# Attention, routed experts and an MLP in one kernel: expert 0's place cut from 160 to 128 rows, and the order of the loads behind it

## The chip, the cores and the metric

One core of a Trainium2 chip runs the whole program. The metric is device time in microseconds of one execution, the median of three runs; the profile is one further execution of the same program, with times in microseconds from the start of its span.

## What is computed

Three stages follow each other. Causal attention with a decay runs over 2 batches of 8 heads, 576 positions and 64 columns. A gate then sends each of the 1152 tokens to one of 8 experts, an MLP of 512 to 1024 to 512 with a relu, and an expert keeps its first 288 tokens. A last MLP of 512 to 2048 to 512 runs over all tokens.

```python
scores = np.where(causal, -1000000000.0, scores + decay)
attn = np.exp(scores - max); attn = attn / (sum + 1e-09)
x = attn @ v                                    # 1152 tokens of 512
expert_idx = np.argmax(x @ w_gate, axis=1)      # 8 experts, capacity 288
h = np.maximum(np.einsum('ecd,edf->ecf', disp, w1), 0.0)
y = np.einsum('ecf,efd->ecd', h, w2)            # out[i] = gate_w[i] * y
h = x @ w_in                                    # then the last MLP
g = np.where(h >= 1, h, np.where(h <= -1, 0.0, (h + 1) ** 2 / 4))
out = g @ w_out
```

With the inputs that the reference draws the gate gives the eight experts 89, 168, 151, 69, 104, 79, 131 and 361 tokens; expert 0 has 89.

## The kernel before

**Attention** (lines 411 to 938) is a loop over steps t, each of which works on several heads at once; a string of operations (ORDER) fixes the order on every engine. In step t the score columns of head t + 1 are made (cols_part, lines 534 to 552: two matmuls, an exp on ACT, and on POOL the mask of the diagonal block, line 551), and head t is multiplied with v (av_part, line 588), which reads the masked blocks of the step before. The helper at line 525 sends a row of corrections through a small DMA, which the matmul at line 547 reads one step later.

**The token buffer.** disp lies in DRAM and holds CAPS rows per expert. It is filled with zeros first: in step t the pieces 2t - 2 and 2t - 1 of 128 rows are written from an SBUF tile (lines 887 to 889), as many pieces as E * CAPS / 128. CAPS comes from the table of places (lines 69 to 75), where RW is the largest number of tokens that can be left over at one place. Then the tokens are scattered into it with indirect DMAs of POOL (scatter, line 729): five for batch 0 in steps 11 to 15, five for batch 1 after the attention.

**The places.** PLACES lists, in the order in which the experts are worked, the rank by size and the rows of a place. Place 0 is always expert 0, whose tokens don't go through disp: perm (line 721; 80 PE matmuls in the trace, two for each f32 product) picks them with one-hot matrices of C0 columns, C0 being the rows of place 0, and lines 935 and 937 copy the result from PSUM into XT. The tokens of the others are read back from disp by x_load (four DMAs, line 407) and turned around by x_trans (DVE, lines 1026 and 1030; for places over 160 rows, "split" ones, ACT makes a rounded copy at line 1031 and DVE or POOL the rest at line 1032).

**The experts** (expert, lines 1139 to 1178). A place goes through eight quarters of weights of 512 KB each. In the four quarters of w1, eight blocks of PSUM columns are made, and ACT writes each through a relu into hf (line 1100), so that one of four PSUM banks is free again. The four quarters of w2 go in eight half products (PARTS); the third of these is the first to read the blocks 4 to 7 of hf. In places of up to 160 rows the matmul at line 1045 reads the weights as they were loaded, in f32; the trace shows 64 matmuls for w1 and 64 for w2 in such a place. x_trans of the next place stands between the blocks of w1 if that place is split (after blocks 1, 3, 5 and 7), else between the half products of w2.

**The loads.** All weights go through the queue of SP, in the order of a list (loads, line 176), each as soon as one of 13 buffers is free: eight RAW and, after the attention, five ST. Eight quarters of place 0 are loaded into RAW during the attention. The list also holds the weights of the last MLP, "m" loads of 512 KB; the first of them stands behind the seventh quarter of place 1, and its conversion, three DVE steps at lines 962, 965 and 968, is tied by m_step to blocks 0, 2 and 4 of place 1. SP works strictly in order, and x_load waits in it until the scatter has landed.

```python
        pump()                                   # line 1093
                if i == 0:                       # lines 1153 to 1156, in expert(e)
                    x_fetch(1)
                if r == 3:
                    x_fetch(e + 2)
```

Of the kernel before, what the change touches and what calls it, by code (L numbers as in the profile page):

```python
# [10 lines left out]
F32 = mybir.dt.float32  # L11
# [4 lines left out]
ACTF = mybir.ActivationFunctionType  # L16
# [8 lines left out]
def most_over(places, n):  # L25
    best = 0
    for m in range(1 << len(places)):
        over = [p for p in range(len(places)) if m >> p & 1]
        need = sum(places[p][1] + 1 for p in over if p == 0)
        for r in range(len(places) - 1):  # L30
            need += max([places[p][1] + 1 for p in over if p and places[p][0] >= r], default=0)
        if need <= n:
            best = max(best, len(over))
    return best
# [3 lines left out]
def attention_moe_mlp_kernel(  # L38
# [14 lines left out]
    nc = tc.nc  # L53
# [6 lines left out]
    KD = DM // 128  # L60
# [3 lines left out]
    KF = 8  # L64
# [1 line left out]
    NG = 3  # L66
    GW = N // NG
    GT = GW // 128
    PLACES = ((7, 160), (6, 128), (0, 288), (5, 128), (1, 224), (4, 128), (2, 192), (3, 160))
    CP = [c for _, c in PLACES]  # L70
    C0, CMAX = CP[0], max(CP)
    PS = [sum(CP[:p]) for p in range(E + 1)]
    LEFT = [min(cap, N // (r + 1) if p else N) - c for p, (r, c) in enumerate(PLACES)]
    RW = max(LEFT) // 32 * 32
    CAPS = max([c + RW for c, o in zip(CP, LEFT) if o > 0] + CP)
    NK = most_over(PLACES, N)
    XW = max([min(N, PS[p]) + CP[p] for p in range(E)] + [N + RW])
    THREE = 256
    SPLIT = [c > 160 for _, c in PLACES]
    NHL = 5  # L80
# [19 lines left out]
    xt_p = ctx.enter_context(tc.tile_pool(name="xtp", bufs=1))  # L100
# [32 lines left out]
    def build_tables(pos_c):  # L133
# [4 lines left out]
        for e in range(E):  # L138
            nc.gpsimd.memset(place_c[:, e], float(PLACES[e][0]))
            nc.gpsimd.memset(cap_c[:, e:e + 1], float(CP[e]))  # L140
# [10 lines left out]
    def quarter_src(i):  # L151
        p, r = divmod(i, 8)
        w = (w1, w2)[r // 4]
        if p == 0:
            return w1[E, r] if r < 4 else w2[0, r - 4]
        return w[bass.ds(at_place(p), 1), r % 4].rearrange("e p f -> (e p) f")
# [3 lines left out]
    def at_place(p):  # L160
        if p not in places:
            places[p] = nc.sync.value_load(ord_i[0:1, p:p + 1], min_val=0, max_val=E - 1)
        return places[p]
# [18 lines left out]
    def pump(n=99):  # L182
        while n and free and loads:
            _, kind, i = loads.popleft()
            t = raws[kind, i] = free.popleft()
            if kind == "w":
                src = quarter_src(i)
            elif kind == "m":
                t, src = t.bitcast(U32), (w_in, w_out)[i % 2][i // 2].bitcast(U32)
            else:  # L190
                src = more_src(i)
            nc.sync.dma_start(out=t, in_=src)
            n -= 1
# [204 lines left out]
        nc.vector.tensor_tensor(out=order_sb, in0=ps[:, NT:], in1=ge[:, 0, 0:NT], op=ALU.add)  # L398

    xrs, xts, x_next = {}, {}, []  # L400
    XT = xt_p.tile([128, KD, C0], F32, tag="xt", name="XT")

    def x_load(e, src):
        n = src.shape[0] // 32
        xrs[e] = x_next[e % 2 if e < E else 1]
        for j in range(DM // 128):
            nc.sync.dma_start(out=xrs[e][32 * j:32 * j + 32, 0:n],
                          in_=src[:, 128 * j:128 * j + 128].rearrange("(t p) d -> p t d", p=32))


    with ExitStack() as actx:
# [179 lines left out]
        def norm_scale(h):  # L591
            o = AV[h % 2][:, :, (h % 2) * (NV - VC):(h % 2) * (NV - VC) + VC]
            r = sm_p.tile([128, IB], F32, tag="r", name="r")
            nc.vector.tensor_scalar(out=r, in0=o[:, :, D + E], scalar1=1e-9, scalar2=None, op0=ALU.add)
            nc.vector.reciprocal(out=r, in_=r)
            return o, r.unsqueeze(2)
# [120 lines left out]
        def perm(b, ibs, ks=range(KD)):  # L717
            for ib in ibs:
                n = min(128, S - ib * 128)
                for k in ks:  # L720
                    nc.tensor.matmul(px[k][:, 0:C0], xss[b][:n, ib, 2 * k:2 * k + 2].rearrange("p h d -> p (h d)"),
                                     sel[b, ib][:n].bitcast(F32), start=((b, ib) == (0, 0)),
                                     stop=((b, ib) == (NB - 1, IB - 1)))

        def scatter(b, ibs):
            si, xs = sis[b], xss[b]
            for ib in ibs:
                n = min(128, S - ib * 128)
                nc.gpsimd.indirect_dma_start(
                    out=disp_v[b * IB + ib], out_offset=bass.IndirectOffsetOnAxis(ap=si[:n, ib:ib + 1], axis=0),  # L730
                    in_=xs[:n, ib].rearrange("p h d -> p (h d)"), in_offset=None,
                    bounds_check=E * CAPS - 1, oob_is_err=False)
# [149 lines left out]
        for t in range(-AHD, NH + 1):  # L882
# [24 lines left out]
            if t == HB + 6:  # L907
                px = [next(s1), next(s1), next(s2), next(s2)]
                s2_free = next(s2)
        o, r = norm_scale(NH - 1)  # L910
# [19 lines left out]
        for k in range(KD):  # L930
            perm(1, range(3, IB), (k,))
        xts[0] = XT
        for k in range(KD):
            if k % 2:
                nc.vector.tensor_copy(out=XT[:, k], in_=px[k][:, 0:C0])
            else:
                nc.scalar.activation(out=XT[:, k], in_=px[k][:, 0:C0], func=ACTF.Copy)
        scatter(1, range(IB))
        bases_gen = compact_bases()

# [34 lines left out]
    def m_step(h):  # L975
        while m_at and m_at[0] <= h:
            m_at.pop(0)
            next(conv)
# [32 lines left out]
    with ExitStack() as mctx:  # L1011
        mp = mctx.enter_context(tc.tile_pool(name="moe", bufs=1))
        x_next.extend(mp.tile([128, max(CP[2 - i::2] + [RW]) // 32, 128], F32, name=f"xn_r{i}")
                      for i in range(2))
        xn = mp.tile([128, KD, 2, CMAX], F32R, name="xn")
        hf = mp.tile([128, KF, C0], F32, name="hf")
        xT0 = mp.tile([128, CMAX], F32, name="xT0")

        def x_trans(e, k, n, split):
            if k == 0:  # L1020
                xts[e] = xn if split else XT if e < E else (
                    x_next[0].rearrange("p t d -> p (t d)")[:, 0:KD * n].rearrange("p (k n) -> p k n", n=n))
# [67 lines left out]
        def more_src(i):  # L1090
            return (w1, w2)[i % 8 // 4][bass.ds(more_e[i // 8], 1), i % 4].rearrange("e p f -> (e p) f")

        pump()
        hx = mp.tile([128, KF, 2, CMAX], F32R, name="hx")
        tp = mctx.enter_context(tc.tile_pool(name="sum", bufs=2))
        invert = invert_slots(px[3][:, 32:32 + 2 * (N // 128)], tp)
# [37 lines left out]
        def x_fetch(e):  # L1134
            if e < E:
                x_load(e, disp.rearrange("(e c) d -> e c d", c=CAPS)[bass.ds(at_place(e), 1), 0:CP[e]]
                       .rearrange("e c d -> (e c) d"))

        def expert(e):
            x, n, split = xts.pop(e), CP[e], SPLIT[e]  # L1140
            for r in range(4):
                i = e * 8 + r
                for fi in range(2):
                    fc = r * 2 + fi
                    ps = bank(ph_ring, n, split)
                    for k in range(KD):
                        c = slice(k * 256 + fi * 128, k * 256 + fi * 128 + 128)
                        product(ps, (hls if split else raws)["w", i], c, operand(x, k, n, split), k == 0, k == KD - 1)
                    hidden(ps, fc, n, split, 2 * i + fi)
                    w_step(2 * i + fi)  # L1150
                    if e + 1 < E and SPLIT[e + 1] and 2 * r + fi in XUP:
                        x_trans(e + 1, XUP.index(2 * r + fi), CP[e + 1], True)
                if i == 0:
                    x_fetch(1)
                if r == 3:
                    x_fetch(e + 2)
                extra(i)
                done("w", i)
            yb = {}
            for s, (d, f0, f1) in enumerate(PARTS):  # L1160
                i = e * 8 + 4 + d
                if f0 == 0:
                    yb[d] = bank(py_ring, n, split)
                for fc in range(f0, f1):
                    c = slice(fc * 128, fc * 128 + 128)
                    product(yb[d], (hls if split else raws)["w", i], c, operand(hx if split else hf, fc, n, split), fc == 0, fc == KF - 1)
                if f1 == KF:
                    token(yb[d], d, n, *bases[e])
                z = 2 * e * 8 + 8 + s
                w_step(z)  # L1170
                m_step(z)
                for k in range(KD):
                    if e + 1 < E and not SPLIT[e + 1] and s == XAT[k]:
                        x_trans(e + 1, k, CP[e + 1], False)
                if s % 2:
                    extra(z // 2)
                if f1 == KF:
                    done("w", i)

        for e in range(E - 2):  # L1180
            expert(e)
        for _ in plan:
# [179 lines left out]
```

## Time and profile before

| | |
|---|---|
| median of three runs | 486.29 us (486.25 to 486.47) |
| the profiled execution | 486.1 us, span 484.4 us, granted clock 0.987 |
| PE busy | 467.2 us, 96% |
| DVE, ACT, POOL busy | 306.0, 257.9, 153.3 us |
| attention with the picking of expert 0's tokens | to 130.4 us |
| place 0, place 1 | 130.4 to 147.9 us, 147.9 to 162.1 us |
| places 2 to 7 | to about 280 us |
| last MLP | to the end |

A busy share says only how full an engine was. What a change of one stage is worth is read from the stage: which engine has no gap in it, and which wait ends last where there is one.

### The profile page before, as it was taken

The page shows a single profiled execution, that of the slowest core. Times are in us where ns is not written, and L with a number is a line of the kernel's source. Part 1 is how long each engine was busy: PE and PEld are TensorE (multiplying, and loading weights), DVE is VectorE, ACT ScalarE, POOL GpSimd, SP SyncE. Part 2 cuts the span into 40 slices and gives each one's busy share as a digit, 9 for nine tenths or more (in the row PEclk, how much of TensorE's full clock was granted, in tenths as well). Part 3 has the DMA queues.
Part 4 walks back from the last instruction along what each step waited for, and adds up shares of the span by engine and source line. Part 5 has one row for each costly group of instructions (what it writes and reads, how often), then busy time and mean ns, then how long its engine had stood idle before and what let it go on. Part 6 is the DMA issues. An engine that isn't in the chain of part 4 may idle for free. (4 is left out here: it accounts for less than half of the span.)

```text
span 484.4 us, 8905 instructions
## 1 busy us (share of the span) xinstructions
PE 467.2 (96%) x3054; PEld 430.3 (89%) x3054; DVE 306.0 (63%) x778; ACT 257.9 (53%) x579; POOL 153.3 (32%) x242
## 2 busy tenths in 40 slices
PE   6799999999999999999998999999999999999995
PEld 2499998999899999999997999999999999999994
DVE  8657768844415666757566268887878554755532
ACT  8867776764224642673561354545455455566650
POOL 7867866763302380292190220000000000400002
PEclk9889999999999999999998999999999999999999
DMA  7558998921569985978970554333300000300001
GB/s 211 164 167 266 321 303 283 292 77 44 170 251 355 369 322 156 354 278 262 300 279 7 207 188 150 118 126 128 127 1 0 1 0 2 130 2 0 1 0 65
DMA packets 38576, 78.46 MB, mean 162 GB/s; under 512 B 14103, under 2 KB 19175, under 8 KB 38524
## 3 DMA queue, kind: packets, MB, share of 16 engines
q1 hardware_dynamic: 37020, 73.19, 45.7%
q0 software_dynamic: 1456, 4.57, 2.4%
q8 instruction: 26, 0.43, 0.4%
q14 instruction: 26, 0.21, 0.1%
q10 hardware_dynamic: 48, 0.06, 0.0%
HBM read 67.36 MB, written 10.49 MB: 161 GB/s over the span
## 5 line engine op out<-in xcount | busy, mean ns | idle before, releaser
L1000 PE MATMUL PB<-x2h,HL 128*128 128x384 f32 x192 | 64.9, 338 | 0.0
L1002 PE MATMUL PB<-x2h,HL 128*128 128x384 f32 x192 | 64.6, 336 | 0.0
L1001 PE MATMUL PB<-x2l,HL 128*128 128x384 f32 x192 | 64.4, 336 | 0.0
L588 PE MATMUL PB<-VT,pt 128*128 128x102 f32 (+2 forms) x480 | 60.5, 262 | 0.0
L588 PEld LDWEIGHTS PB<-VT,pt 128*128 128x128 f32 (+2 forms) x480 | 55.1, 175 | 3.9
L1269 DVE SCALAR_TENSOR_TENSOR PB<-PB,s 128x384 f32<-128x384 f32 x48 | 27.2, 566 | 48.5 <-ACT s L1267 45.9
L1284 PE MATMUL PB<-HL,gh 128*128 128x512 f32 x144 | 56.6, 393 | 0.0
L1283 PE MATMUL PB<-HL,gh 128*128 128x512 f32 x144 | 56.4, 392 | 0.0
L1285 PE MATMUL PB<-HL,gl 128*128 128x512 f32 x144 | 56.0, 389 | 0.0
L1266 ACT ACTIVATE s<-PB 128x384 f32<-128x384 f32 x48 | 23.6, 492 | 56.5 <-PE PB L1002 55.7
L548 ACT ACTIVATE pt<-PB 128x288 f32<-128x288 f32 (+2 forms) x96 | 35.7, 391 | 25.3 <-PE PB L547 22.6
L1290 POOL DMA_INDIRECT out_dram<-ST,order_sb x6 | 6.0, 997 | 133.1 <-DVE ST L1289 131.6
L514 DVE CUSTOM_DVE_ANT_0 dump<-PB,msk 128x128 f32<-128x128 f32 (+1 forms) x64 | 30.9, 490 | 21.7 <-PE PB L508 19.1
L1270 ACT ACTIVATE gh<-PB 128x384 fp32r<-128x384 f32 x48 | 23.6, 492 | 32.8 <-DVE PB L1269 31.7
L1000 PEld LDWEIGHTS PB<-x2h,HL 128*128 128x128 f32 x192 | 36.1, 188 | 1.8
L1001 PEld LDWEIGHTS PB<-x2l,HL 128*128 128x128 f32 x192 | 36.0, 188 | 1.8
L1002 PEld LDWEIGHTS PB<-x2h,HL 128*128 128x128 f32 x192 | 36.0, 188 | 0.0
L508 PE MATMUL PB<-KB,QM 128*128 128x128 f32 (+2 forms) x96 | 31.8, 348 | 3.9 <-DVE KB L796 3.2
L1272 DVE TENSOR_TENSOR gl<-PB,gh 128x384 fp32r<-128x384 f32 x48 | 26.8, 558 | 13.4 <-ACT gh L1270 13.4
L546 PE MATMUL PB<-QA,KA 128*128 128x288 f32 (+2 forms) x96 | 31.1, 327 | 1.4 <-ACT pt L548 1.1
L1285 PEld LDWEIGHTS PB<-HL,gl 128*128 128x128 f32 x144 | 27.0, 188 | 6.0
L997 DVE TENSOR_TENSOR HL<-wc,HL 128x512 fp32r<-128x512 f32 x40 | 27.0, 719 | 7.9 <-ACT HL L996 7.9
(295 smaller groups left out, 1125.3 us busy)
## 6 DMA issues: line engine op xcount, KB each, us to landing
RAW<-in_w_dram SPq DMA_DIRECT2D x40, 512.0 KB
ST<-in_w_dram SPq DMA_DIRECT2D x24, 512.0 KB
qk<-in_qkT_dram SPq DMA_DIRECT2D x15, 576.0 KB
RAW<-in_w_in_dram SPq DMA_DIRECT2D x12, 512.0 KB
disp<-zero SPq DMA_DIRECT2D x22, 256.0 KB
RAW<-in_w_out_dram SPq DMA_DIRECT2D x9, 512.0 KB
ST<-in_w_out_dram SPq DMA_DIRECT2D x7, 512.0 KB
VT<-in_v_dram SPq DMA_DIRECT2D x8, 320.0 KB
```

Of the source, the lines that this page charges most:

```text
L508: nc.tensor.matmul(s[:n, :w - a], QM[h % 2][:, ib * 128:ib * 128 + n], KB[i][:, a:w], start=True, stop=True)
L514: nc.vector.tensor_tensor_reduce(out=dump[:n, :w - a], in0=s[:n, :w - a], in1=msk[:n, m0:m0 + w - a], scale=1.0, scalar=NEG if r < IB else ...
L546: nc.tensor.matmul(s[:n, :z - a], KA[i][:, js], QA[i][:, iss], start=True, stop=False)
L548: nc.scalar.activation(out=pt[:n, POFF[jb] + a:POFF[jb] + z], in_=s[:n, :z - a], func=ACTF.Exp, scale=0.125)
L588: nc.tensor.matmul(o[:n, ib, ws], pt[:m, c0:c0 + n], v[:m, jb].rearrange("p a b -> p (a b)")[:, vs], start=(jb == 0), stop=(jb == ib))
L1000: nc.tensor.matmul(ps, wh, ah, start=first, stop=False)
L1001: nc.tensor.matmul(ps, wh, al, start=False, stop=False)
L1002: nc.tensor.matmul(ps, wl, ah, start=False, stop=last)
L1269: nc.vector.scalar_tensor_tensor(out=ps, in0=ps, scalar=1.0, in1=s, op0=ALU.max, op1=ALU.min)
L1283: nc.tensor.matmul(o, gh[:, c], wh, start=(fc == 0), stop=False)
L1284: nc.tensor.matmul(o, gh[:, c], wl, start=False, stop=False)
L1285: nc.tensor.matmul(o, gl[:, c], wh, start=False, stop=(fc == NF2 - 1))
```

## The change

Place 0 has 128 rows in place of 160. XT and hf keep the size of 160 columns, for place 7. Of the loads that the queue takes when the ST buffers become free, only three are issued first (the quarters 0 to 2 of place 1), then the tokens of place 1, then those of place 2, and only then the other two quarters; the reads of the tokens out of the loop of place 0 are dropped.

```diff
-    PLACES = ((7, 160), (6, 128), (0, 288), (5, 128), (1, 224), (4, 128), (2, 192), (3, 160))
+    PLACES = ((7, 128), (6, 128), (0, 288), (5, 128), (1, 224), (4, 128), (2, 192), (3, 160))
     CP = [c for _, c in PLACES]
-    C0, CMAX = CP[0], max(CP)
+    C0, CMAX, CF = CP[0], max(CP), max(c for c in CP if c <= 160)
...
-    XT = xt_p.tile([128, KD, C0], F32, tag="xt", name="XT")
+    XT = xt_p.tile([128, KD, CF], F32, tag="xt", name="XT")
...
-                nc.vector.tensor_copy(out=XT[:, k], in_=px[k][:, 0:C0])
+                nc.vector.tensor_copy(out=XT[:, k, 0:C0], in_=px[k][:, 0:C0])
             else:
-                nc.scalar.activation(out=XT[:, k], in_=px[k][:, 0:C0], func=ACTF.Copy)
+                nc.scalar.activation(out=XT[:, k, 0:C0], in_=px[k][:, 0:C0], func=ACTF.Copy)
...
-        hf = mp.tile([128, KF, C0], F32, name="hf")
+        hf = mp.tile([128, KF, CF], F32, name="hf")
...
-        pump()
+        pump(3)
...
-                if i == 0:
-                    x_fetch(1)
-                if r == 3:
+                if r == 3 and e:
                     x_fetch(e + 2)
...
+        x_fetch(1)
+        x_fetch(2)
+        pump()
         for e in range(E - 2):
             expert(e)
```

The table also sets RW, and through it CAPS. Before, the largest rest was 128 (the capacity of 288 less 160 at place 0), so RW was 128 and CAPS 224 + 128 = 352, which makes 22 pieces of zeros. Now the largest rest is 288 - 128 = 160, CAPS is 384, and there are 24 pieces. The last two fall in step 12, and the first scatter is in step 11.

SP's queue in steps 11 and 12 of the attention, before (disp is the token buffer, ct the row of corrections; DMASW is a semaphore of a scatter, DMAHW of a DMA of SP):

```order
L889 DMA disp<-zero 128x512 [waits DMAHW5_49]
L525 DMA QB_151<-ct 1x5x128 [waits DMAHW6_49,Activation_49]
L467 DMA VT_160<-in_v_dram 128x10x64 [waits DMAHW7_49,PE_49]
L525 DMA QB_152<-ct 1x5x128 [waits DMAHW0_49,Activation_49]
L162 TENSOR_LOAD ord_i [waits DVE_49]
```

and now:

```order
L889 DMA disp<-zero 128x512 [waits DMAHW5_49]
L525 DMA QB_151<-ct 1x5x128 [waits DMAHW6_49,Activation_49]
L467 DMA VT_160<-in_v_dram 128x10x64 [waits DMAHW7_49,PE_49]
L889 DMA disp<-zero 128x512 [waits DMAHW0_49,DMASW0_49]
L889 DMA disp<-zero 128x512 [waits DMAHW1_49]
L525 DMA QB_152<-ct 1x5x128 [waits DMAHW2_49,Activation_49]
L162 TENSOR_LOAD ord_i [waits DVE_49]
```

Two writes of zeros stand ahead of the row of corrections, and the first waits for a scatter. On POOL the same stretch reads now (before, the second L729 waited for ACT alone):

```order
L496 TENSOR_TENSOR QB_152<-qk,QA_144 64x576 [waits Activation_49,Pool_49]
L551 AFFINE_SELECT pt<-pt 128x128 [waits Activation_49] x4
L551 AFFINE_SELECT pt<-pt 64x64 [waits Activation_49]
L729 DMA disp<-xs,si 3072x512 [waits DMAHW1_49,DMAHW0_49,Activation_49]
L471 COPY VT_160<-vwall 128x10x8
```

The second scatter waits for the two writes of zeros (DMAHW0 and DMAHW1), and behind it in POOL's order stand the copy into VT and the masks of the next head.

SP's queue behind the attention, now (xn_r of 32x4x128 are the tokens of place 1, of 32x9x128 those of place 2; in_w_dram is an expert's weights, in_w_in_dram the first m load):

```order
L192 DMA ST_1752<-in_w_dram 128x1024 [waits DMAHW5_49]
...
L407 DMA xn_r_1781<-disp 32x4x128
...
L407 DMA xn_r_1780<-disp 32x9x128
...
L192 DMA ST_1753<-in_w_dram 128x1024 [waits DMAHW6_49]
L192 DMA ST_1754<-in_w_dram 128x1024 [waits DMAHW7_49]
L192 DMA RAW_100<-in_w_dram 128x1024 [waits DMAHW0_49,PE_49]
L192 DMA RAW_101<-in_w_dram 128x1024 [waits DMAHW1_49,PE_49]
L192 DMA RAW_102<-in_w_in_dram 128x1024 [waits DMAHW2_49,PE_49]
L192 DMA RAW_103<-in_w_dram 128x1024 [waits DMAHW3_49,PE_49]
```

Before, five ST loads stood ahead of the tokens of place 1, then two RAW loads and the m load, and only then the tokens of place 2. So between the tokens of place 1 and the m load there were two loads, and now there are the tokens of place 2 and four loads.

The order of DVE in place 1 is the same in both programs (now):

```order
L1127 TENSOR_TENSOR x2l<-PB_74,x2h 128x128 [waits Activation_49]
L236 TENSOR_TENSOR mm<-at,base_f 128x64
L239 TENSOR_REDUCE bx<-mm 128x8 [waits DVE_49]
L962 TENSOR_SCALAR wc_1763<-RAW_102 128x512 [waits DMASW6_49,DMASW7_49,DMASW5_49,DMAHW2_49,DMASW1_49,DMASW0_49]
L1030 STREAM_TRANSPOSE xT_1784<-xn_r_1780 128x288 [waits DMAHW5_49,DMAHW4_49,DMAHW3_49]
L1032 TENSOR_TENSOR xn<-xT_1784,xn 128x288 [waits Activation_49]
```

The first step on the m load (L962, of RAW_102) stands ahead of the first turning of place 2's tokens (L1030).

## Rows read from the trace of the kernel before

**Rows 1.** The page's line of engines: busy us (share of the span) and instructions.

```profile
PE 467.2 (96%) x3054; PEld 430.3 (89%) x3054; DVE 306.0 (63%) x778; ACT 257.9 (53%) x579; POOL 153.3 (32%) x242
```

**Rows 2.** Waits of PE from 30 us on: us in total, times, longest.

```profile
PE PB L1045 <- PEq L1228: 2.2, 1, 2.2
PE PB L508 <- DVE STAT L514: 0.4, 1, 0.4
```

**Rows 3.** PE's timeline, places 0 and 1: start us, us, engine, line, operation, count.

```profile
130.40 8.96 PE L1045 MATMUL PB<-XT,RAW 128*128 128x160 f32 x64
139.20 8.86 PE L1045 MATMUL PB<-hf,RAW 128*128 128x160 f32 x64
147.89 7.31 PE L1045 MATMUL PB<-XT,ST 128*128 128x128 f32 x64
```

**Rows 4.** Stretches: length; busy (count) of PE, PEld, DVE, ACT, POOL; clock; DMA share; GB/s.

```profile
117.29:120.57 3.28, 3.28 (x26) 3.25 (x25) 2.33 (x14) 1.61 (x7) 0.00 (x0) 1.00 0.00 1
130.40:147.89 17.49, 17.49 (x130) 17.49 (x129) 4.26 (x23) 3.34 (x11) 1.38 (x2) 1.00 0.79 286
147.89:162.10 14.21, 14.21 (x131) 14.21 (x129) 10.82 (x26) 8.00 (x21) 2.79 (x4) 1.00 1.05 368
```

**Rows 5.** POOL's timeline in steps 11 to 13 (in brackets the idle time before).

```profile
100.39 1.17 POOL L729 DMA_INDIRECT disp<-xs,si  x1 [0.29 <-POOL QB L496]
104.50 0.99 POOL L729 DMA_INDIRECT disp<-xs,si  x1 [0.59 <-ACT ct L524]
105.68 0.33 POOL L551 TENSOR_SCALAR_AFFINE_SELECT pt<-pt 128x128 f32<-128x128 f32 x1
```

**Rows 6.** The scatter issued at 104.50 us, by itself.

```profile
DMA to landing us min/median/max: 2.8/2.8/2.8
```

**Rows 7.** A stretch of step 13, columns as in rows 4.

```profile
105.00:106.00 1.00, 1.00 (x10) 0.97 (x8) 0.86 (x3) 0.98 (x3) 1.00 (x3) 1.00 0.06 20
```

**Rows 8.** SP's timeline (x is the number of DMAs in the row).

```profile
93.64 0.92 SPq L889 DMA_DIRECT2D disp<-zero  x2
125.77 2.53 SPq L192 DMA_DIRECT2D ST<-in_w_dram  x5
139.17 1.89 SPq L407 DMA_DIRECT2D xn_r<-disp  x4
143.58 1.87 SPq L407 DMA_DIRECT2D xn_r<-disp  x4
```

**Rows 9.** PE's timeline, step 14: the product with v that follows the first score columns.

```profile
109.36 0.36 PE L588 MATMUL PB<-VT,pt 128*128 128x102 f32 x2
```

**Rows 10.** The last scatter: POOL's timeline, and its landing by itself.

```profile
131.18 0.91 POOL L729 DMA_INDIRECT disp<-xs,si  x1 [0.30 <-issue]
...
DMA to landing us min/median/max: 7.7/7.7/7.7
```

**Rows 11.** Stretches behind the attention, columns as in rows 4.

```profile
131.00:137.00 6.00, 6.00 (x46) 6.00 (x45) 1.10 (x7) 1.52 (x5) 0.91 (x1) 1.00 1.02 406
139.00:140.00 1.00, 1.00 (x9) 1.00 (x8) 0.00 (x0) 0.30 (x1) 0.00 (x0) 1.00 0.00 0
147.00:150.00 3.00, 3.00 (x27) 3.00 (x26) 1.15 (x4) 0.65 (x3) 0.00 (x0) 1.00 1.17 236
```

**Rows 12.** DVE's timeline in place 1.

```profile
149.24 0.43 DVE L962 TENSOR_SCALAR wc<-RAW 128x512 uint32<-128x512 uint32 x1
150.54 0.69 DVE L1030 STREAM_TRANSPOSE xT<-xn_r 128x288 f32<-128x288 f32 x1 [0.88 <-DMA xn_r<-disp]
```

**Rows 13.** ACT's timeline in place 1.

```profile
151.27 0.44 ACT L1031 ACTIVATE xn<-xT 128x288 fp32r<-128x288 f32 x1 [1.06 <-DVE xT L1030]
155.86 0.45 ACT L1100 ACTIVATE hf<-PB 128x128 f32<-128x128 f32 x2 [0.16 <-ACT xn L1031]
```

**Rows 14.** Stretches around PE's one long gap, columns as in rows 4.

```profile
257.46:259.70 2.24, 0.01 (x1) 0.03 (x1) 2.17 (x7) 0.33 (x1) 0.00 (x0) 1.00 0.01 4
260.55:263.96 3.41, 3.41 (x14) 2.83 (x13) 1.23 (x3) 0.47 (x2) 0.00 (x0) 0.50 0.01 2
```

## The prediction, made before the changed kernel was run

> **What bounds the kernel now.** I read the page's line of engines first, to see whether one engine is the bound: PE is busy 467.2 us, 96% of the span [rows 1]. The waits of PE come next, to see what it ever waits for: from 30 us on there is one wait of 2.24 us and one of 0.4 [rows 2]. So a matmul that gets shorter counts in full, unless something that was hidden comes late; a change here is judged by what it makes late. PE's timeline of places 0 and 1 shows streams without a hole, 64 matmuls for each of w1 and w2 [rows 3], at full clock [rows 4]. Then I follow the two queues that the change rearranges: POOL and SP in attention steps 12 and 13 [rows 5, 8], and SP, DVE and ACT behind the attention [rows 8, 12, 13].
>
> The sum is made against the profiled execution, 486.1 us; the median of the runs is 486.29, about 0.2 above it, which is added at the end. A difference under 0.2%, about 1 us, can't be told from none.
>
> **The gain.** Place 0 takes 17.49 us for 128 matmuls of 160 columns, 136.6 ns each, and place 1 takes 14.21 us for 128 of 128 columns, 111.0 ns [rows 4]. The difference, 25.6 ns, times 128 is 3.3 us. In the picking of expert 0's tokens 26 matmuls take 3.28 us [rows 4], 126 ns each; a fifth of that is 25 ns, times 80 is 2.0 us. PE is full in both stretches, so the gain is **-5.3 us** if nothing comes late. The copies into XT shrink with the columns, some hundredths of a microsecond, taken as nothing. Expert 0 has 89 tokens, so its rest stays empty in both programs.
>
> **Cost 1: two more writes of zeros, in the attention.** CAPS grows to 384, and the writes of zeros of step 12 wait for scatter 0, as the order of SP shows. That scatter was issued at 100.39 [rows 5]. How long it takes has no row of its own here; another one took 2.8 us and the last one, beside weight loads, 7.7 [rows 6, 10], so it lands between 103.2 and 108.1. I take 106, the middle, since in its stretch one load and the end of the zeros share the DMA engines. The pair of writes then takes 0.92 us to issue [rows 8], the second about 0.5 behind the first, and lands 2.6 us after its issue at about 109.1; that is a little under the 2.8 us of a transfer of the same 256 KB [rows 6], for hardly anything else moves then, 20 GB/s [rows 7]. The second scatter on POOL waits for both. It can go at about 109.4 and not at 104.50 [rows 5], 4.9 us late, and the copy and the masks stand behind it. The first mask went at 105.68 for 0.33 us; 4.9 later it ends at 110.9. PE wants it for the product with v at 109.36 [rows 9]. So PE stands still for about **+1.7 us** (with the scatter at 103.2: 0, since the mask would end at 108.1; with it at 108.1: 3.8). The row of corrections that stands behind the writes in SP's queue goes out at about 107.1 and not before the first score columns of step 14 need it by much; its lateness lies inside the same 1.7 us. Batch 0's later scatters and the masks behind them are late by the same amount at first, and POOL has idle time in each step to catch up; I cost that at nothing.
>
> **Cost 2: the m load behind the tokens of place 2.** In SP's queue the reads of the tokens wait for the last scatter, issued at 131.18, landed 7.7 us later, at 138.9 [rows 10]; SP went on at 139.17 [rows 8], 0.3 behind. While it waited the queue moved 406 GB/s [rows 11]: five ST loads and the scatters. Now two loads of 512 KB fewer stand there, 1.05 MB / 406 GB/s = 2.6 us, and the picking is some 0.6 us shorter up to that scatter, so it lands at 135.7, counted on the old clock of the attention (bounds: neither helps, 138.3; both and the shorter picking in full, 133.4). The tokens of place 1 are issued from 136.0, for 1.9 us, and those of place 2 start at 138.2 [rows 8]. Their first bytes come 1.4 us after that; this is an estimate from the stretch behind the issue at 139.17, in which nothing has moved yet by 140.00 [rows 11]. Their 590 KB take 2.5 us at the 236 GB/s at which the tokens went before [rows 11]. Five loads follow, the fifth of them the m load, at 524 KB / 406 GB/s = 1.29 us each, 6.5 in all. So the m load lands at 148.6.
>
> This estimate of the link rests on the 406 GB/s of the trace. The Trainium skill, DMA: Bandwidth & Descriptors, Where 436 GB/s comes from, says that a transfer from HBM to SBUF is bound at the HBM side, at some 358 GB/s. By that rule each load would take 1.46 us, the m load would come 0.9 us later, and the sum would be 0.9 us higher; the trace moves 406 here, and the measurement decides.
>
> Before, the m load was there when DVE reached line 962 at 149.24, in place 1's first matmuls, and the first turning of place 2's tokens came at 150.54, held by those tokens [rows 12]. Now the tokens come early and the m load late. Place 1 starts 5.3 us earlier, at 142.6, and its six first blocks of w1, 7.31 us / 8 = 0.89 a block at their rate [rows 3], are done at 147.9. Only four banks exist: the seventh block needs the bank of the third, which ACT empties behind the copy of line 1031 [rows 13], which needs DVE's turning of line 1030, which stands behind line 962. DVE can do line 962 at 148.6, for 0.43 us, and the turning at 149.0. Before, the last block of w1 was emptied 5.8 us after the turning (150.54 to 155.86 + 0.45 [rows 12, 13]); the third of the eight half products reads it. Six half products of 0.89 us are 5.3. So place 1 ends at about 149.0 + 5.8 + 5.3 = 160.1, where it ended at 162.10 [rows 4] and would end at 156.8 with the gain alone. This costs **+3.3 us**, and one for one with the landing of the scatter (bounds +1.0 and +5.9). PE's first gap there is about 2.4 us, from 147.9 to ACT's emptying at some 150.3. If the attention is late by cost 1, the scatter, the m load and place 1 all move by that, and nothing is counted twice. Later weights are asked for in the same order, and place 2 keeps its tokens; I cost the rest at nothing, since PE ran without a wait from place 2 to 257 us before [rows 2].
>
> **The clock.** After PE's one long gap, 2.24 us, the granted clock is 0.50 for 3.41 us, and 14 matmuls run there [rows 14]. At half the full 2.4 GHz the stretch does half its work, so it costs 1.7 us. The 0.4 us gap was not followed by that. The two new gaps, 1.7 and 2.4 us, stand near the one that was; I count one such stretch, **+1.7 us** (bounds 0 and 3.4).
>
> **Sum.** -5.3 + 1.7 + 3.3 + 1.7 = +1.4; 486.1 + 1.4 = 487.5, and 0.2 for the median: **487.7 us**.
>
> **The rivals.**
> - *Both waits, no stretch at half clock*: -5.3 + 1.7 + 3.3 = -0.3, 486.0 us. For it: the gaps may be shorter than estimated, or fall where the chip does not answer. Chance 0.25.
> - *Both gaps are followed by one*: 487.7 + 1.7 = 489.4 us. Chance 0.10.
> - *Faster, since the m load isn't late*: it decides whether the last scatter lands by about 133 instead of 135.7. Its 7.7 us [rows 10] against the 2.8 of one by itself [rows 6] say that the loads in the queue hold it; with two fewer it could gain more than their own time. Then only cost 1 is left and with it perhaps a stretch at half clock: -5.3 + 1.7 = -3.6, 482.7, or 484.4 us. Against it: three loads still stand ahead. Chance 0.15.
> - *Faster, since the zeros don't hold POOL*: if scatter 0 lands at 103.5 or before, the masks are in time. Then -5.3 + 3.3 = -2.0, 484.3 us, or 486.0 with a stretch. Chance 0.13, a third of it with the stretch.
> - *Neither is late*: 486.3 - 5.3 = 481.0 us. Chance 0.07.
> - *The change doesn't do what it says*: expert 0 would overflow its 128 rows and go through the rest's loop; with 89 tokens it can't here. No chance is given to it.
>
> **How the numbers follow.** The forecast has 0.30. Faster by over 1 us: 0.15 + 0.08 + 0.07 = 0.30. The same: 0.25 + 0.05 = 0.30. Slower: 0.30 + 0.10 = 0.40. The forecast's own range, with the landing of the scatter 1 us either way, is 486.7 to 488.7. The range for 8 in 10 leaves out the case in which neither is late and most of that of two stretches: 482.6 to 489.0.
>
> **What would show it.** PE's timeline of place 0 should show 64 matmuls in about 7.3 us; if not, the gain fails. In the waits of POOL the second scatter should stand at about 109 with a wait for the writes of zeros, and PE should wait at line 588 for the masks. In place 1 DVE should wait at line 962 for the m load, PE at line 1045 for ACT's relu, and the windows should show a granted clock of 0.50 behind one of the gaps. The forecast is wrong if place 1's m load is in RAW before its first blocks are done, if POOL's second scatter goes at about 104, or if no stretch at half clock follows.

## The result, and the profile after

The changed kernel takes **489.30 us** (489.06 to 489.41, four runs) against 486.28 before: ratio 1.0066, 95% interval 1.0048 to 1.0083. It is slower by 3.0 us, where 487.7 was forecast with a range up to 489.0. The direction was right, the size was not, and the range ended 0.3 us too early. A second measurement, with runs of the kernel before on the same chip beside it, gives 488.85 us and 1.0053 (1.0036 to 1.0069). The profiled execution took 489.06 us, span 487.4, against 486.1 and 484.4. Executions of one and the same kernel differ here by up to some 5 us (484.6 to 489.4 for the kernel before), and the traces show stretches at half clock in one execution that another lacks, so medians are compared, and stretches of the traces beside them.

PE's waits from 30 us on, changed kernel (us in total, times, longest); before there were only the two of [rows 2] of this size:

```profile
PE PB L1045 <- ACT hf L1100: 4.9, 1, 4.9
PE PB L1045 <- PEq L1229: 2.1, 1, 2.1
PE PB L588 <- POOL pt L551: 1.6, 1, 1.6
PE PB L1045 <- issue: 0.7, 1, 0.7
PE PB L508 <- DVE STAT L514: 0.4, 1, 0.4
```

Both forecast waits are there, 1.6 us at line 588 behind POOL's masks and 4.9 us at line 1045 behind ACT's relu. (L1229 is the branch that was L1228 in the program before.)

The whole program in stretches, first the kernel before and then the changed one: up to the picking of expert 0's tokens, the picking, place 0, place 1 (the last two of before are in [rows 4]), places 2 to 6, and what follows the branch. Columns as in [rows 4].

```profile
0.00:117.29 117.29, 108.51 (x855) 94.22 (x856) 78.63 (x282) 82.74 (x186) 83.30 (x176) 0.97 0.69 220
117.29:130.40 13.11, 13.11 (x94) 11.35 (x92) 6.51 (x34) 5.04 (x13) 3.43 (x4) 1.00 0.26 72
162.10:257.46 95.36, 94.62 (x718) 92.55 (x716) 63.81 (x163) 49.36 (x127) 47.95 (x44) 1.00 0.81 276
259.70:478.98 219.28, 219.28 (x1137) 200.45 (x1137) 139.15 (x246) 109.09 (x220) 12.82 (x12) 0.99 0.20 66
```

```profile
0.00:118.25 118.25, 109.51 (x855) 93.93 (x856) 78.67 (x282) 82.78 (x186) 82.84 (x176) 0.97 0.70 222
118.25:129.40 11.15, 11.15 (x93) 9.93 (x92) 6.38 (x34) 4.99 (x13) 2.45 (x3) 1.00 0.19 53
129.40:143.93 14.53, 14.53 (x130) 14.47 (x130) 3.94 (x23) 3.05 (x11) 2.35 (x3) 1.00 0.66 213
143.93:165.84 21.91, 17.04 (x130) 16.84 (x129) 10.66 (x26) 7.93 (x21) 2.77 (x4) 0.84 1.03 381
165.84:261.31 95.47, 94.72 (x718) 92.65 (x716) 63.89 (x163) 49.32 (x127) 47.97 (x44) 1.00 0.79 267
263.43:481.97 218.54, 217.86 (x1137) 199.16 (x1137) 139.22 (x246) 109.09 (x220) 12.81 (x12) 1.00 0.20 66
```

Line by line the differences are +0.96, -1.96, -2.96, **+7.70** (21.91 against the 14.21 of [rows 4]), +0.11, -0.12 for the gap at the branch, and -0.74: together +2.99. One stretch, place 1, takes more than the gains give; the rest is small.

PE in places 0 and 1, changed kernel (start us, us, engine, line, operation, count, and in brackets the idle time before):

```profile
129.40 7.41 PE L1045 MATMUL PB<-XT,RAW 128*128 128x128 f32 x64
136.65 7.44 PE L1045 MATMUL PB<-hf,RAW 128*128 128x128 f32 x64
143.93 5.52 PE L1045 MATMUL PB<-XT,ST 128*128 128x128 f32 x48
154.32 3.78 PE L1045 MATMUL PB<-XT,ST 128*128 128x128 f32 x16 [4.87 <-ACT hf L1100]
157.90 1.91 PE L1045 MATMUL PB<-hf,ST 128*128 128x128 f32 x8
```

Six blocks (48 matmuls) go, then PE stands still for 4.87 us, and the last two blocks take 3.78 us where two took 1.8 at full clock. DVE says why, in the same stretch:

```profile
152.61 0.43 DVE L962 TENSOR_SCALAR wc<-RAW 128x512 uint32<-128x512 uint32 x1 [7.45 <-DMA RAW<-in_w_in_dram]
152.95 0.68 DVE L1030 STREAM_TRANSPOSE xT<-xn_r 128x288 f32<-128x288 f32 x1
```

DVE waits 7.45 us for the first m load, with the turning of place 2's tokens directly behind it; in [rows 12] the turning stood at 150.54 and waited for the tokens themselves. SP's queue in that part, to be held against [rows 8]:

```profile
126.01 1.48 SPq L192 DMA_DIRECT2D ST<-in_w_dram  x3
137.29 4.54 SPq L407 DMA_DIRECT2D xn_r<-disp  x8
142.02 0.89 SPq L192 DMA_DIRECT2D ST<-in_w_dram  x2
143.16 0.91 SPq L192 DMA_DIRECT2D RAW<-in_w_dram  x2
144.18 0.37 SPq L192 DMA_DIRECT2D RAW<-in_w_in_dram  x1
```

Five stretches of the same part: while the tokens are issued, while place 2's tokens land, while their bytes move (by the packets of the trace), while the five loads land, and the clock behind the gap.

```profile
137.30:141.20 3.90, 3.90 (x37) 3.90 (x36) 0.24 (x1) 0.55 (x2) 0.00 (x0) 1.00 0.25 71
141.20:144.70 3.50, 3.50 (x32) 3.44 (x31) 2.42 (x15) 0.56 (x2) 0.00 (x0) 1.00 1.03 253
140.95:143.85 2.90, 2.90 (x27) 2.84 (x27) 2.40 (x13) 0.28 (x1) 0.00 (x0) 1.00 1.00 225
144.70:150.00 5.30, 4.75 (x43) 4.56 (x41) 0.42 (x3) 0.56 (x2) 0.00 (x0) 1.00 1.03 407
152.91:159.73 6.82, 5.41 (x25) 5.41 (x26) 5.52 (x12) 3.68 (x10) 2.77 (x4) 0.50 1.03 410
```

SP takes 4.54 us to issue the eight reads of tokens and issues no load meanwhile, and the DMA engines are a quarter busy, 71 GB/s, for 3.9 us of it. Then everything that place 1 waits for comes at once. One packet of an instruction queue comes among the loads; in the window from 147.2 to 148.5 us (queue and kind, packets, MB, share of the time of 16 engines):

```profile
q8 instruction: 1, 0.02, 5.3%
```

The attention part: POOL's second scatter in the changed kernel, and then PE at its wait, to be held against [rows 5, 9].

```profile
99.45 1.16 POOL L729 DMA_INDIRECT disp<-xs,si  x1 [0.30 <-POOL QB L496]
...
108.67 0.99 POOL L729 DMA_INDIRECT disp<-xs,si  x1 [5.70 <-ACT xs L654]
```

```profile
110.22 0.47 PE L588 MATMUL PB<-VT,pt 128*128 128x102 f32 x2 [1.63 <-POOL pt L551]
```

The second scatter comes 9.2 us behind the first; before it was 4.1. The releaser that the profile names, ACT, had long been done; in the order the instruction waits for the two writes of zeros, which SP issued at 105.11:

```profile
105.11 0.82 SPq L889 DMA_DIRECT2D disp<-zero  x2
```

### The profile page after: what moved, and what is told of

The parts are those of the page before. It is cut to its first block, busy times and chain, and to the rows that moved or that the text cites. A ratio compares the mean times of both kernels' runs of the same rounds, so it can differ in the third digit from the quotient of the medians.

```text
span 487.4 us, 8908 instructions
## 1 busy us (share of the span) xinstructions
PE 464.8 (95%) x3054; PEld 427.0 (88%) x3054; DVE 305.5 (63%) x778; ACT 257.5 (53%) x579; POOL 152.8 (31%) x242
```

## The experiments

The runs come from two chips. The kernel before has a median of 486.36 us on the one (zeros earlier, m load's step later, old order, new order with 160 rows) and of 486.22 on the other (the rest), and the changed kernel's 488.85 is from the other.

**The changed kernel again**, without an edit.

> The changed kernel itself, on the same chip as the runs beside it, as their measure. Theory (the loss lies in waits that the program's order sets): 0.6% above the kernel before, with PE's two gaps of about 1.6 and 4.9 us. Rival (the first measurement caught this kernel in a bad phase of the granted clock): within 0.2% of the kernel before.

Measured: 488.85 us, ratio to before 1.0053 (1.0036 to 1.0069). The loss is real. In this profile PE's two waits are 0.9 and 4.8 us:

```profile
PE PB L1045 <- ACT hf L1100: 4.8, 1, 4.8
PE PB L1045 <- PEq L1229: 2.2, 1, 2.2
PE PB L588 <- POOL pt L551: 0.9, 1, 0.9
```

The wait in place 1 comes back at its size; the one in the attention is smaller, since the zeros were issued 4.9 us behind the first scatter and not 5.7. Place 1 took 20.86 us here, with one stretch of 3.4 us at half clock where the first profile had 6.8:

```profile
144.45:165.31 20.86, 16.10 (x130) 15.91 (x129) 10.65 (x26) 7.93 (x21) 2.77 (x4) 0.92 1.03 386
```

**The zeros earlier.**

```diff
-            for z in range(2 * t - 2, 2 * t):
+            for z in range(2 * t, 2 * t + 2):
```

> The changed kernel with each pair of zero writes one step earlier, so that the last pair is in step 11, ahead of the first scatter. Theory (the zeros held POOL and PE): the second scatter on POOL goes about 4 us behind the first one and not 9.2, PE's wait of 1.63 us for the masks at line 588 is gone, and the rest moves up with it: 489.3 less 1.6 to 1.9, 487.4 to 487.7 us. Rival (the wait only moves, since place 1 waits for a load whose time is set elsewhere): 489.0 to 489.5, with a longer wait in place 1.

Measured: 487.9 us, ratio 1.003 (1.0008 to 1.0052), 1.0 us under the changed kernel's 488.85 and 1.4 under its first 489.30. The mechanism is as the theory says, on POOL:

```profile
100.34 1.17 POOL L729 DMA_INDIRECT disp<-xs,si  x1 [0.30 <-POOL QB L496]
...
104.45 0.99 POOL L729 DMA_INDIRECT disp<-xs,si  x1 [0.59 <-ACT ct L524]
```

4.1 us again, as in [rows 5], and PE has no wait at line 588. Place 1 has its gap still, 4.8 us. The trace shows the mechanism; the size of the saving is less sure. It is 1.0 us here and 2.0 between the two kernels with the m load's step later, below, but the changed kernel and this one were measured on two chips and their intervals overlap, and so it is, by a little, with that pair.

**The m load's step later.**

```diff
-    m_at = place(3 * MCONV, ..., lambda h: h >= 16 and h % 16 in MRES[SPLIT[h // 16]])
+    m_at = place(3 * MCONV, ..., lambda h: h >= 16 and h % 16 in (MRES[1][:3] if h < 32 else MRES[SPLIT[h // 16]]))
...
-                         [(m_at[3 * j] - 0.5, "m", j) for j in range(MCONV)]))
+                         [(m_at[3 * j] - 0.5 if j else 15.5, "m", j) for j in range(MCONV)]))
```

> The changed kernel with the first m load's three DVE steps tied to the second half of place 1 (slots 10, 12 and 14) in place of blocks 0, 2 and 4; the order of the loads is as in the changed kernel. Theory (place 1 stood still because DVE waited for the m load at line 962 ahead of the turning of place 2's tokens): the gap of 4.87 us and the clock stretch behind it go, place 1 takes 14.3 us and not 21.9, and the time is 489.3 - 7.6 = 481.7 us (481 to 483). Rival (the tokens of place 2 or a weight load come next as the late one): place 1 still has a gap of 2 us or more, 484 us or above.

Measured: 483.23 us, ratio 0.9939 (0.9917 to 0.9960): 5.6 us under the changed kernel's 488.85, and faster than before. Place 1, in one window:

```profile
144.53:158.74 14.21, 14.21 (x130) 14.21 (x129) 8.73 (x21) 8.05 (x21) 2.80 (x4) 1.00 1.02 401
```

No gap, full clock, 14.21 us to the hundredth of [rows 4]. The tokens of place 2 and the weights were not late; only the m load was. The 7.6 us expected became 5.6. Held against the changed kernel's second profile, place 1 gives 20.86 - 14.21 = 6.65; behind the branch this execution has a half-clock stretch that the other one lacks, some 0.7 us, and small differences of 0.2 to 0.4 us lie at the branch and in the attention.

**The old order of loads, with 128 rows.**

```diff
-        pump(3)
+        pump()
...
-                if r == 3 and e:
+                if i == 0:
+                    x_fetch(1)
+                if r == 3:
                     x_fetch(e + 2)
...
-        x_fetch(1)
-        x_fetch(2)
-        pump()
```

> The changed kernel (place 0 of 128 rows) with the loads and token reads in the order of before. Theory: the m load is early again, but the tokens of place 2 land some 11.6 us behind the last scatter, at about 151, so DVE turns them at 151 and not at 152.95: a gap of 2 to 3 us in place 1 is left, 486.5 to 488 us. Rival (the new order is what makes 128 rows bearable, and the old order is worse): 489.5 us or above. Rival (the order alone made the loss): 483 to 484 us.

Measured: 485.78 us, ratio 0.9998 (0.9982 to 1.0016), 3.1 us under the changed kernel. No expectation had the place right. Windows of places 0 and 1, and PE's waits:

```profile
128.43:147.07 18.64, 16.18 (x129) 15.99 (x129) 3.90 (x23) 3.05 (x11) 2.37 (x3) 0.91 0.78 286
147.07:161.28 14.21, 14.21 (x130) 14.21 (x129) 10.39 (x25) 7.99 (x21) 2.79 (x4) 1.00 1.05 368
```

```profile
PE PB L1045 <- DVE x2l L1127: 2.5, 1, 2.5
PE PB L1045 <- PEq L1228: 2.1, 1, 2.1
PE PB L588 <- POOL pt L551: 0.6, 1, 0.6
```

Place 1 has no gap. The wait stands in **place 0**, now 3 us shorter than it was. DVE holds the writing of a result (line 1127) behind the turning of place 1's tokens:

```profile
142.61 0.69 DVE L1026 STREAM_TRANSPOSE XT<-xn_r 128x128 f32<-128x128 f32 x2 [12.36 <-DMA xn_r<-disp]
...
143.32 0.48 DVE L1127 TENSOR_TENSOR x2l<-PB,x2h 128x128 fp32r<-128x128 f32 x2
```

So the new order did mend something: it brings place 1's tokens in time for a place 0 of 128 rows. In these traces that is worth about 4 us (18.64 against 14.53): 2.5 us of wait, and most of the rest a stretch of 3.4 us at half clock behind it (the granted clock of place 0 is 0.91). It then loses 7.7 in place 1.

**The new order, with 160 rows.** On the kernel before:

```diff
-        pump()
+        pump(3)
...
-                if i == 0:
-                    x_fetch(1)
-                if r == 3:
+                if r == 3 and e:
                     x_fetch(e + 2)
...
+        x_fetch(1)
+        x_fetch(2)
+        pump()
```

> The kernel before (place 0 of 160 rows, 22 writes of zeros) with the new order of loads and token reads alone. Theory: the m load lands at about 152 and not at 147.65, line 962 holds the turning of place 2's tokens until about 152.5 and not 150.54, and place 1 ends 1 to 2 us later: 487.3 to 488.5 us. Rival (place 0 of 160 rows gives the loads enough time): 486.0 to 486.6 us.

Measured: 485.71 us, ratio 0.9997 (0.9982 to 1.0012), no difference. The theory is refuted; the rival comes nearest, though its 486.0 to 486.6 us lie a little above the measured time.

```profile
151.60 0.43 DVE L962 TENSOR_SCALAR wc<-RAW 128x512 uint32<-128x512 uint32 x1 [2.43 <-DMA RAW<-in_w_in_dram]
```

```profile
147.88:162.53 14.65, 14.65 (x130) 14.36 (x129) 10.30 (x25) 8.02 (x21) 2.79 (x4) 1.00 1.04 399
```

DVE waits 2.43 us for the m load, as the theory says, but place 1 is longer by only 0.44 us. Place 1 starts at 147.88, and its first six blocks, which need no bank that waits for the turning, take until about 153.2 (an estimate, six times 0.89 us, a sixteenth of 14.21). The same order is harmless or costs 7.7 us, by when place 1 begins.

**The m load two places earlier** (behind five weight loads and not seven).

```diff
-                         [(m_at[3 * j] - 0.5, "m", j) for j in range(MCONV)]))
+                         [(m_at[3 * j] - (0.5 if j else 4.5), "m", j) for j in range(MCONV)]))
```

> The changed kernel with the first m load two places earlier in SP's queue (behind five weight loads in all and not seven); its DVE steps stay in blocks 0, 2 and 4 of place 1. Theory (the gap follows the landing of the m load one for one): the load lands 2 x 1.27 = 2.5 us earlier, the gap in place 1 falls from 4.9 to 2.3 us, place 1 takes 18 to 19.5 us with a clock stretch and 17 without, the time falls by 2.5 to 4.5 us against the changed kernel. Rival (the tokens, or the weights behind, hold place 1): the gap stays at 4 us or more.

Measured: 485.44 us, ratio 1.0001 (0.9971 to 1.0031), 3.4 us under the changed kernel beside it.

```profile
PE PB L1045 <- ACT hf L1100: 2.3, 1, 2.3
```

```profile
143.14:160.14 17.00, 14.73 (x130) 14.36 (x129) 10.25 (x25) 7.99 (x21) 2.78 (x4) 1.00 1.02 404
```

4.8 less two loads of 1.27 us is 2.3. DVE went on at line 962 at 149.22, 6.08 us after the start of place 1, where the changed kernel's first profile has 8.68, and the gap is 2.27 us against 4.87: it follows the landing one for one. This gap, 2.3 us, was not followed by half clock.

**PE kept busy in the gap.**

```diff
                     ps = bank(ph_ring, n, split)
+                    if e == 1 and fc == 6:
+                        for _ in range(24):
+                            nc.tensor.matmul(px[1][:, 0:512], ones_b, ones_b.unsqueeze(1).to_broadcast([128, 4, 128]),
+                                             start=True, stop=True)
```

> The changed kernel with 24 matmuls of 512 columns on constants (their result isn't used) on PE ahead of the seventh block of place 1, about 5.1 us of work in the place where PE stood still for 4.9. Theory (the stretch at half clock that followed that gap cost about 1.9 us by itself): the granted clock stays 1.00 there, place 1 takes about 20.2 us and not 21.9, 1.5 to 1.9 us faster than the changed kernel. Rival (the stretch cost nothing, since place 1 waits for ACT and DVE anyway): the same as the changed kernel, or 0.2 to 0.5 us slower by the added work.

Measured: 487.02 us, 1.8 us under the changed kernel beside it, though it does 24 matmuls more.

```profile
150.17 5.34 PE L1148 MATMUL PB<-ones_b 128*128 128x512 bf16 x24
155.35 1.95 PE L1045 MATMUL PB<-XT,ST 128*128 128x128 f32 x16
```

```profile
144.81:164.36 19.55, 19.55 (x154) 16.71 (x153) 10.30 (x25) 7.97 (x21) 2.77 (x4) 1.00 1.04 391
```

The window of place 1 is 19.55 us at a granted clock of 1.00, and the two blocks behind the gap take 1.95 us and not 3.78. Against the changed kernel's profiles that is 2.4 us less than the first (6.8 us at half clock) and 1.3 less than the second (3.4 us). By the medians about 1.8 us of the loss are the clock's, and useless work gets them back.

**Both repairs**, the zeros earlier and the m load's step later.

> The changed kernel with both repairs: each pair of zero writes one step earlier, and the first m load's DVE steps in the second half of place 1. Theory (the two costs are independent): 483.2 less 1.3 to 1.9, 481.3 to 482.0 us, and PE has no wait over 0.5 us between 30 us and the long gap at about 253. Rival (they cover each other, or a new wait takes their place): 483 us or above.

Measured: **481.20 us**, ratio 0.9898 (0.9865 to 0.9931), the fastest of all: 1.0% under the kernel before, and 2.0 us under the kernel with the m step alone. PE's waits from 30 us on:

```profile
PE PB L1045 <- PEq L1229: 2.4, 1, 2.4
PE PB L508 <- DVE STAT L514: 0.4, 1, 0.4
```

Of the larger waits only those of the kernel before are left. 486.22 - 481.20 = 5.0 us is what place 0's 32 columns give when nothing comes late; 5.3 was forecast.

## Why the prediction was right or wrong

- **The gain, -5.3 us: right.** The picking gave 1.96 and place 0 2.96, together 4.9, and the kernel with both repairs is faster by 5.0.
- **Cost 1, +1.7 us: the mechanism right, the size at the upper end of what occurs.** PE's wait is 1.63 us in the profile. From the first scatter to the picking 18.80 us pass against 16.90. Moving the zeros removed the wait. The forecast had scatter 0 land at 106 and POOL go on at 109.4. In the changed kernel the zeros went at 105.11, 5.7 behind the scatter's issue, and POOL went on 9.2 behind it where 9.0 was forecast. In the six traces that keep 128 rows and these zeros the zeros go 4.6 to 5.7 us behind the first scatter, and PE's wait goes with it one for one, from 0.6 to 1.6 us; that this profile drew the longest is luck.
- **Cost 2, +3.3 us: the mechanism right, the size wrong. This is the step that failed: the term that puts the m load's landing at 148.6.** DVE waited at line 962, the turning stood behind it, ACT emptied the bank late, PE stopped after the sixth block: all as written. But the m load came later. Forecast: 6.0 us after the start of place 1 (148.6 against 142.6). Measured: 152.61 against 143.93, 8.7 us. The scatter's end was right: the tokens were issued 6.6 us ahead of place 1, and 136.0 against 142.6 was forecast. Place 2's first bytes were right too, at 140.95, 3.0 us ahead of place 1. Their 590 KB took 2.9 us and not 2.5, and the bytes of the five loads ended, counted in packets, at 150.62, 6.8 us behind them and not 6.5. The largest part, 2.0 us, lies between those last bytes and DVE's start at 152.61. The forecast had nothing for it: it let a load be there when its bytes had moved.
- **Inside those 2.0 us.** The trace records sixteen landings for each load, and DVE goes on 0.1 us behind the last of the m load's. Those of the first two loads lie within 0.3 and 0.5 us. Those of the m load come between 150.72 and 151.42, except for the sixteenth, at 152.49. The spread begins with the third load, when the packet of the instruction queue takes 1.1 us, from 147.32 on. In the run with the new order at 160 rows this packet comes only at 151.62. There the m load's sixteen landings lie within 0.8 us, and DVE goes on 1.2 us behind its last bytes (150.44 and 151.60). So some 0.8 of the 2.0 us seem to go with that packet; no run moved it by itself, and its part is argued, not shown.
- **What the late landing did.** The gap was 4.9 us where 2.4 was forecast. From the turning to the last block 5.7 us passed (5.8 forecast), so nothing but the landing was off, and the kernel with the load two places earlier shows that the gap goes with it one for one. Without the clock the wait cost 5.3 us (the 19.55 of the run with PE kept busy, less 14.21).
- **The clock, +1.7 us: a stretch came, and its size is near by luck.** One stretch of 3.4 us was counted, wherever it fell. It fell behind place 1's gap and lasted 6.8 us, 1.4 of them still in the gap. Against the window with PE kept busy it cost 2.4 us in this profile (21.91 less 19.55), and 1.3 in the second one, where it lasted 3.4; the medians of the changed kernel and of that run differ by 1.8. The attention's wait was followed by none.
- **What nobody had in the sum.** The first part of the program was 0.9 us shorter up to the first scatter (99.45 against 100.39). The difference arises at about 30 us, behind stretches at half clock that fall differently in the two executions: one of 6.8 us from about 21.5 us on before, two of 3.4 from about 9.5 and 23 now. The branch at 261 us was not followed by half clock this time, and the part behind it is 0.7 us shorter. That both are the clock's is read from these two traces and was not tested.
- **The sum.** Measured by stretches: -4.9 + 1.9 + 5.3 + 2.4 - 0.9 - 0.7 and 0.0 for the rest come to +3.0 before rounding, against +1.4 forecast. Here 5.3 and 2.4 are the two parts of place 1's 7.7. Cost 2 was 2.0 us too small, the clock 0.7, and cost 1 and the gain were 0.2 and 0.4 off to the same side; the two terms that nobody had gave 1.6 back.
- **Slips in the working.** By its own rows cost 1 is 110.9 - 109.36 = 1.5 us and not 1.7. 7.31 us / 8 is 0.91 and not 0.89, which is a sixteenth of 14.21. The bound 133.4 doesn't follow from the terms named beside it: 138.9 less 2.6 and less 2.0 is 134.3, and the lower bound of cost 2 would be +1.9. None of these makes the miss.
- **The rivals.** The one with two half-clock stretches has the right time, 489.4, by the wrong road: it has a stretch behind each new gap and cost 2 at 3.3 us, and there was a stretch behind one gap only, and cost 2 was larger. Those in which a wait does not come did not happen. The order of loads alone was not asked about; it is worth nothing at 160 rows and mends a wait at 128 that the forecast didn't see.

On the link the forecast weighed the Trainium skill, DMA: Bandwidth & Descriptors, Where 436 GB/s comes from, with its 358 GB/s from HBM, against the 406 of the trace. The changed kernel moved 407 while the five loads landed: the measurement holds, and the lateness of the m load isn't that rule's.

## What to carry to other kernels

When a stage gets shorter, look for the loads and steps that had just fitted into it: each of two orders of the same queue was harmless behind a place of 160 rows and cost 4 to 8 us behind one of 128. A step for far later work (here the conversion of a weight of the last MLP, which begins over 100 us later) must not stand in an in-order engine ahead of a step that the next block waits for; moving it by half a place was worth 5.6 us. A derived size, like the rows of a zeroed buffer, can add two small transfers at the one place where the queue meets a dependence.

## What was not expected of the hardware

- Gaps of nearly the same length were answered differently by the clock. After the branch, PE's wait of 2.24 us was followed by 3.4 us at half clock in the kernel before, and one of 2.1 in the changed kernel by none; a gap of 2.3 us in place 1 by none, and the gap of 4.8 or 4.9 by 3.4 us in one execution and by 6.8 in two others. A single profile can't say what a gap costs in clock.
- Small pieces kept the DMA engines as busy as large ones and moved fewer bytes: 225 GB/s at a DMA share of 1.00 while place 2's tokens moved in packets of 512 bytes, against 407 GB/s at 1.03 for loads of 512 KB, in packets of 4 KB. The 236 GB/s of before [rows 11] had shown as much.
- The last of a load's sixteen landings can come 1.1 us behind the other fifteen, as with the m load, and the engine that waits for the load waits for that one.
